# Last products of a three-layer kernel: VectorE's list in another order

## The chip, the cores and the metric

The kernel runs on one core of one Trainium2 chip. The metric is device time in microseconds (us): the time before is the median of three runs. A profile of one further execution shows what each engine of the core did: TensorE (PE, matrix products), VectorE (DVE), ScalarE (ACT), GpSimd (POOL) and SyncE (SP, which issues most DMAs).

## The reference, cut to what matters

```python
q, k, v: (4, 8, 576, 64)      # attention, each row keeps its 32 highest scores
x: (2304, 512)                # its output, then 8 experts of 512 -> 1024 -> 512, the best one per token
def _moe2_ref(x, w_in, w_out, alpha):          # w_in (512, 2048), w_out (2048, 512)
    h = x @ w_in
    g = np.maximum(h, 0.0) + alpha * np.minimum(h, 0.0)
    return (g @ w_out).astype(np.float32)
```

The change touches only this last layer. Its weights arrive in float64 and are turned into float32 on the chip.

## The kernel before

Every float32 operand of a product is held as two tiles, a high part and a low part. ScalarE writes the high part (a copy that rounds), and VectorE or GpSimd subtracts it from the source for the low part. This pair of instructions is called a *split* here. A product is then three matmuls: high by high, high by low, low by high.

The last layer is `last_products`. The 2304 tokens are 9 columns of 256, and the 2048 hidden units are two halves, so there are 18 *groups*, k = 0 to 17: groups 0 to 8 take the first half of the hidden units, groups 9 to 17 the second half. A group has 15 *slots* of 12 matmuls on TensorE:

- eight slots f0 to f7, each of which makes 128 hidden units of the group (`first`): 4 steps d over the 512 inputs, 3 matmuls each. ScalarE (line 1272) and VectorE (line 1273) then apply the slope `alpha`; the pair is called *gg* with its slot's number.
- seven slots for the products of the group before with `w_out`: its 2 by 2 blocks are multiplied with seven products (numbers 1 to 7) and some sums, not with eight. `A[m]` is the split left operand, `B[m]` the split weights of product m. VectorE adds the results (line 1328).

The slots stand in the order `MIXED`: f0, f1, 1, f2, f3, 6, f4, 7, f5, 5, f6, f7, 4, 2, 3. Group 0 has only its eight f slots. Six PSUM banks go round the slots, so a slot needs the bank of six slots earlier to be read out.

Each engine works off its own list in the order of the code; nothing is re-ordered at run time. Around the slots the lists hold:

- the *halves* (lines 1238, 1239): at the end of a group, the split of the next group's input columns, in four pieces; TensorE's next f0 needs the first of them. They stand after gg7, and the last three product slots 4, 2 and 3 run meanwhile.
- the *sums* of a group (lines 1292 to 1295, three instructions on VectorE, after the halves), and s3 (line 1400, at f5); their splits make the `A` tiles (lines 1287 and 1288, the second part on GpSimd).
- `tick`: in groups 1 to 8 it converts 16 pieces of the second half's float64 weights, two pieces a group: four instructions on VectorE (lines 827 to 831), one on GpSimd (line 936). In group 0 it makes the last three splits of `B`.
- `idi`, the token numbers as integers: loaded by a DMA and cast by VectorE in group 0 (line 1385), read by the scatters of the output (line 1315) from group 10 on.
- the *renewal* for the second half: `V`, the split of `w_in`, is written again (`wide_half`, its columns 0 to 511 for slots f0 to f3, 512 to 1023 for f4 to f7), and so are the seven `B` blocks (`new_block`), four of which come from sums of weights (lines 954 to 957, in the order 5, 6, 4, 7).

## Time and profile before

| | before |
|---|---|
| median of 3 runs, us | 1175.03 (1172.89 to 1176.27) |
| the profiled execution: its own time, us | 1173.9 |
| its span, first to last instruction, us | 1172.2 |
| TensorE busy in the span | 1117.1 us, 95% |
| mean granted clock of TensorE (1 is full) | 0.984 |

Times in the rows below are us from the span's start. The profiled execution is 1.1 us below the median of the runs.

### The profile page before, as it was taken

How to read it: one execution, taken by the hardware profiler on the slowest of the kernel's cores; microseconds unless marked ns; L12 is line 12 of the kernel's file. 1: busy time of each engine (PE TensorE's matmuls, PEld its weight loads, DVE VectorE, ACT ScalarE, POOL GpSimd, SP SyncE). 2: the span in 40 equal slices, each digit the busy share in tenths (PEclk: the TensorE clock that was granted, in tenths of full speed). 3: DMA queues.
4: the chain of work that ended last, by engine and by line, in shares of the span. 5: the costliest groups of instructions: out<-in, count | busy, mean ns of one | idle time of the engine just before them, and what ended most of it. 6: DMA issues, size and time to landing. Idle time of an engine off the chain costs nothing.

```text
span 1172.2 us, 28154 instructions
## 1 busy us (share of the span) xinstructions
PE 1117.1 (95%) x9785; PEld 1066.2 (91%) x9785; DVE 872.3 (74%) x3658; ACT 746.0 (64%) x1621; POOL 721.6 (62%) x694
## 2 busy tenths in 40 slices
PE   6999999999999999889999999979999989999996
PEld 4899898899888988889999999979999979999995
DVE  6999989998999899675564666667767797544543
...
GB/s 174 127 131 148 82 78 85 112 79 77 87 85 55 53 26 147 90 189 199 225 191 210 208 247 208 41 101 89 114 92 90 72 46 64 91 73 55 117 30 39
DMA packets 127134, 129.78 MB, mean 111 GB/s; under 512 B 72654, under 2 KB 95182, under 8 KB 126982
## 3 DMA queue, kind: packets, MB, share of 16 engines
...
q0 software_dynamic: 2912, 9.46, 2.2%
q8 instruction: 79, 1.29, 0.5%
q14 instruction: 73, 0.60, 0.2%
...
## 4 chain that ended last, share of the span: by engine, by line
PE 64%; DVE 18%; ACT 9%; issue 4%; DMA 3%; POOL 2%; SPq 0%; POOLq 0%; DVEq 0%; ACTq 0%
PE mm L1327 14%; PE mm L1069 12%; PE mm L1070 11%; PE mm L1068 11%; PE po L345 6%; DVE cand L214 5%; PE s L191 3%; DVE w L236 3%; PE pt L323 2%; ACT sg L285 2%; DVE xT L1239 2%; ACT ss L204 2%; PE pt L324 1%; ACT pT L329 1%; DMA yt<-y 1%
## 5 line engine op out<-in xcount | busy, mean ns | idle before, releaser
L1069 PE MATMUL mm<-xT,wt 128*128 128x256 f32 (+7 forms) x852 | 250.2, 294 | 10.2 <-DVE xT L1239 6.8
L1068 PE MATMUL mm<-xT,wt 128*128 128x256 f32 (+7 forms) x852 | 248.6, 292 | 9.2 <-ACT xT L1238 5.2
L296 POOL TENSOR_TENSOR sg<-ss,sg 128x576 f32<-128x576 f32 x143 | 202.0, 1414 | 84.4 <-ACT sg L285 76.7
L1070 PE MATMUL mm<-xT,wt 128*128 128x256 f32 (+7 forms) x852 | 248.2, 291 | 0.0
L214 DVE MAX8 cand<-ss 128x8 f32<-128x82 f32 (+1 forms) x1008 | 232.3, 234 | 20.0 <-ACT ss L204 19.7
L345 PE MATMUL po<-vt,pT 116*128 116x130 f32 x1440 | 196.2, 282 | 7.4 <-ACT pc L377 6.5
L1327 PE MATMUL mm<-wt,hT 128*128 128x256 f32 x1512 | 193.9, 282 | 0.9 <-POOL hT L1288 0.9
L345 PEld LDWEIGHTS po<-vt,pT 116*128 116x128 f32 x1440 | 172.3, 190 | 22.9 <-ACT pc L377 11.1
L1327 PEld LDWEIGHTS mm<-wt,hT 128*128 128x128 f32 x1512 | 186.2, 191 | 1.1 <-POOL hT L1288 1.1
L1069 PEld LDWEIGHTS mm<-xT,wt 128*128 128x128 f32 x852 | 163.9, 192 | 12.9 <-DVE xT L1239 9.3
L1068 PEld LDWEIGHTS mm<-xT,wt 128*128 128x128 f32 x852 | 163.9, 192 | 9.8 <-ACT xT L1238 5.4
L1070 PEld LDWEIGHTS mm<-xT,wt 128*128 128x128 f32 x852 | 164.0, 192 | 0.0
L323 PE MATMUL pt<-ident,e 128*116 128x128 f32 x720 | 137.5, 275 | 0.7 <-DVE enH L562 0.6
L993 POOL TENSOR_TENSOR wt<-raw,wt 128x1024 fp32r<-128x1024 f32 x29 | 74.7, 2579 | 84.1 <-ACT wt L992 82.3
L285 ACT ACTIVATE sg<-ss,w 128x576 f32<-128x576 f32 x144 | 119.5, 830 | 3.3 <-DVE w L227 2.8
L290 ACT ACTIVATE e<-ss,sm 128x576 f32<-128x576 f32 x144 | 118.7, 824 | 0.1
L191 PE MATMUL s<-kt,qq 64*128 64x144 f32 (+1 forms) x1280 | 113.6, 315 | 5.0 <-ACT ss L204 4.4
L204 ACT ACTIVATE ss<-s 128x576 f32<-128x576 f32 x144 | 102.5, 712 | 14.9 <-PE s L191 9.7
L236 DVE MAX8 w<-sg 128x8 f32<-128x576 f32 x144 | 107.3, 745 | 2.4 <-POOL sg L296 2.1
L1288 POOL TENSOR_TENSOR hT<-wa,hT 128x512 fp32r<-128x512 f32 x36 | 46.5, 1292 | 101.5 <-ACT hT L1287 101.5
L936 POOL TENSOR_TENSOR wf<-wa,raw 128x512 f32<-128x512 f32 x32 | 43.4, 1358 | 99.3 <-DVE raw L831 79.1
L191 PEld LDWEIGHTS s<-kt,qq 64*128 64x128 f32 (+1 forms) x1280 | 80.8, 182 | 24.2 <-ACT ss L204 6.8
...
## 6 DMA issues: line engine op xcount, KB each, us to landing
...
```

What stands on the lines that cost most here:

```text
L191: nc.tensor.matmul(s[to, g, c * n:c * n + n], t["qq"][of, h, q0:q0 + m], t["k"][of, h * HALF + c * n:h * HALF + c * n + n], start=True, st ...
L204: nc.scalar.activation(T.ss.rearrange("p (g s) -> p g s", g=2), T.sv, AF.Copy)
L214: blocks.append(lambda i=i: nc.vector.max(A.cand[:, i], A.ss[:, i * BW:(i + 1) * BW if i + 1 < KB else S]))
L236: fin = [lambda: nc.vector.max(C.w[:, 24:32], C.z), lambda: nc.vector.scalar_tensor_tensor(scr, self.vsel, C.c1, C.w[:, 23:32, None].to_br ...
L285: nc.scalar.activation(T.sg, T.ss, AF.Sign, bias=T.w[:, 23:24], scale=-ABOVE, accum_out=T.c1)
L296: eng.tensor_tensor(T.z, T.ss, T.sg, op=OP.mult)
L323: nc.tensor.matmul(o, T.e[:, c * CK:(c + 1) * CK], self.ident, is_transpose=True, start=True, stop=False)
L345: nc.tensor.matmul(po[:, i:i + 2, :], T.pT[:, c], rhs, start=(c == 0), stop=(c == NCK - 1))
L1068: nc.tensor.matmul(ps, wh, xh, start=first, stop=False)
L1069: nc.tensor.matmul(ps, wh, xl, start=False, stop=False)
L1070: nc.tensor.matmul(ps, wl, xh, start=False, stop=last)
L1327: nc.tensor.matmul(ps, a[:, x, c], b[:, y, c], start=c == r == 0, stop=c == 3 and r == 2)
```

## The change

Four things move; nothing is computed differently, and no instruction of the last layer is added or dropped.

- The cast of the token numbers goes from group 0, f0 to group 1, f0.
- `tick` in group 0 makes its three `B` splits at f2, f4 and f6, not at f2, f5 and f7. In groups 1 to 8 the two weight conversions stand at f1 and f5, not at f3 and f7.
- The renewal of `V` is taken apart: the first columns at f4 and f5 of group 8 (all at f3 before), the second at f0 and f1 of group 9 (all at f7 of group 8, ahead of the sums, before).
- The four sums of weights stand at f0, f2, f4 and f6 of group 9 (all at f0 before), and the splits of the `B` blocks, each right behind the product that last reads the old block before, stand at f3 (B1), f5 (B6) and f6 (B7) of group 9 and at f0 (B5), f2 (B4), f4 (B2) and f6 (B3) of group 10. B1, B6, B7, B2 and B3 are subtracted on GpSimd, B5 and B4 on VectorE (before: B1, B5 and B2 on GpSimd, the other four on VectorE).

```diff
@@ -1273,7 +1273,7 @@
             v.scalar_tensor_tensor(gg, gg, rest[:, 8 * h + f:8 * h + f + 1], ps, op0=OP.mult, op1=OP.add)
             if h == 0:
                 self.n = n1 if g else n0
-                self.tick((g - 1) * 8 + f if g else f, (ng - 1) * 8 if g else 8)
+                self.tick((g - 1) * 8 + (f + 2) % 8 if g else f if f < 7 else -1, (ng - 1) * 8 if g else 7)
             else:
                 self.tick(-1, 1)
 
@@ -1347,21 +1347,29 @@
                 add(at(0, 1), at(0, 1))
                 store(k, 0, 1)
 
-        def wide_half(c):
+        def upper(d, c):
             cs = slice(c * 512, (c + 1) * 512)
-            for d in range(4):
-                t = self.V[d]
-                act.activation(t[:, 0, cs], self.wf[:, d, cs], AF.Copy)
-                (pool if d % 2 else v).tensor_tensor(t[:, 1, cs], self.wf[:, d, cs], t[:, 0, cs].bitcast(F32), op=OP.subtract)
-
-        def new_block(m):
-            if m == 0:
-                for i in (4, 5, 6, 7):
-                    raws[i] = self.wk.tile([P, 4, G2], F32, name="raw", bufs=4)
-                for i, f in self.sums(lambda i: raws[i]):
-                    f()
-                return
-            self.split_block(m, raws[m] if m >= 4 else self.quarter(m), pool if m in (1, 5, 2) else v)
+            t = self.V[d]
+            act.activation(t[:, 0, cs], self.wf[:, d, cs], AF.Copy)
+            (pool if d % 2 else v).tensor_tensor(t[:, 1, cs], self.wf[:, d, cs], t[:, 0, cs].bitcast(F32), op=OP.subtract)
+
+        def new_sum(j):
+            if not raws:
+                raws.update((i, self.wk.tile([P, 4, G2], F32, name="raw", bufs=4)) for i in (5, 6, 4, 7))
+            self.sums(raws.get)[j][1]()
+
+        def new_block(m, eng):
+            self.split_block(m, raws[m] if m >= 4 else self.quarter(m), eng)
+
+        RENEW = {}
+        for d in range(4):
+            RENEW.setdefault((ng - 1, 4 + d // 2), []).append(lambda d=d: upper(d, 0))
+            RENEW.setdefault((ng, d // 2), []).append(lambda d=d: upper(d, 1))
+        for j, f in enumerate((0, 2, 6, 4)):
+            RENEW.setdefault((ng, f), []).append(lambda j=j: new_sum(j))
+        for m, k, f, eng in ((1, 0, 3, pool), (6, 0, 5, pool), (7, 0, 6, pool), (5, 1, 0, v), (4, 1, 2, v), (2, 1, 4, pool),
+                             (3, 1, 6, pool)):
+            RENEW.setdefault((ng + k, f), []).append(lambda m=m, eng=eng: new_block(m, eng))
 
         x = self.load_columns(1)
         for k in range(last + 1):
@@ -1372,8 +1380,6 @@
                 if isinstance(s, int):
                     if k:
                         product(p, s)
-                        if k == ng:
-                            new_block(s)
                     continue
                 f = int(s[1])
                 first(k, t, f)
@@ -1382,9 +1388,8 @@
                         split(5, quarter(p, 1, 0))
                     else:
                         nc.sync.dma_start(ids, self.idc[:NT].rearrange("(t p) -> p t", p=P))
+                    if k == 1:
                         v.tensor_copy(idi, ids)
-                    if k == ng:
-                        new_block(0)
                 if f == 1 and k:
                     split(4, quarter(p, 1, 1))
                 if f == 2 and k:
@@ -1393,8 +1398,6 @@
                     if k:
                         split(3, quarter(p, 0, 0))
                     split(1, quarter(k, 0, 0))
-                    if k == ng - 1:
-                        wide_half(0)
                 if f == 5:
                     s3 = new()
                     v.tensor_tensor(s3, quarter(k, 0, 0), quarter(k, 1, 0), op=OP.subtract)
@@ -1405,9 +1408,9 @@
                     if k < last:
                         t = self.halves(x)
                         x = self.load_columns((k + 2) % ng if k + 2 <= last else ng)
-                    if k == ng - 1:
-                        wide_half(1)
                     sums(k)
+                for renew in RENEW.get((k, f), ()):
+                    renew()
         k = last
         split(5, quarter(k, 1, 0))
         split(4, quarter(k, 1, 1))
```

The first place is VectorE's list in group 0. `xr`, `hT` and `alpha` in the rows of line 1273 are gg; line 967 is the split of a `B` block, line 1239 the halves, line 1400 (1403 in the change) s3. Before:

```order
L1273 SCALAR_TENSOR_TENSOR xr<-xr,alpha,mm 128x256
L1385 CAST idi<-idf 128x18
L1273 SCALAR_TENSOR_TENSOR xr<-xr,alpha,mm 128x256 x2
L967 TENSOR_TENSOR wt<-wf,wt 128x1024
L1273 SCALAR_TENSOR_TENSOR xr<-xr,alpha,mm 128x256
L1273 SCALAR_TENSOR_TENSOR hT<-hT,alpha,mm 128x256 x2
L1400 TENSOR_TENSOR wa<-xr 128x512
L1273 SCALAR_TENSOR_TENSOR hT<-hT,alpha,mm 128x256 x2
L967 TENSOR_TENSOR wt<-wf,wt 128x1024
L1239 TENSOR_TENSOR xT<-xr,xT 128x256 x4
```

and with the change:

```order
L1273 SCALAR_TENSOR_TENSOR xr<-xr,alpha,mm 128x256 x3
L967 TENSOR_TENSOR wt<-wf,wt 128x1024
L1273 SCALAR_TENSOR_TENSOR xr<-xr,alpha,mm 128x256
L1273 SCALAR_TENSOR_TENSOR hT<-hT,alpha,mm 128x256 x2
L1403 TENSOR_TENSOR wa<-xr 128x512
L1273 SCALAR_TENSOR_TENSOR hT<-hT,alpha,mm 128x256
L967 TENSOR_TENSOR wt<-wf,wt 128x1024
L1273 SCALAR_TENSOR_TENSOR hT<-hT,alpha,mm 128x256
L1239 TENSOR_TENSOR xT<-xr,xT 128x256 x4
```

The cast is gone from behind gg0, the first `B` split stays behind gg2, and the last one stands ahead of gg7 instead of behind it.

The second place is VectorE's list at the end of group 1, as in groups 2 to 7: lines 827 to 831 are a weight conversion, `y<-mm` the additions of product results. Before:

```order
L1273 SCALAR_TENSOR_TENSOR wt<-wt,alpha,mm 128x256
L1400 TENSOR_TENSOR wa<-wt 128x512
L1328 TENSOR_TENSOR y<-mm,y 128x256 x2
L1273 SCALAR_TENSOR_TENSOR wt<-wt,alpha,mm 128x256 x2
L827 TENSOR_SCALAR wa<-raw 128x512
L828 SCALAR_TENSOR_TENSOR wa<-raw,wa 128x512
L829 TENSOR_SCALAR raw<-wa 128x512
L831 SCALAR_TENSOR_TENSOR raw<-raw 128x512
L1239 TENSOR_TENSOR xT<-xr,xT 128x256 x4
```

and with the change:

```order
L1273 SCALAR_TENSOR_TENSOR wt<-wt,alpha,mm 128x256
L827 TENSOR_SCALAR wa<-raw 128x512
L828 SCALAR_TENSOR_TENSOR wa<-raw,wa 128x512
L829 TENSOR_SCALAR raw<-wa 128x512
L831 SCALAR_TENSOR_TENSOR raw<-raw 128x512
L1403 TENSOR_TENSOR wa<-wt 128x512
L1328 TENSOR_TENSOR y<-mm,y 128x256 x2
L1273 SCALAR_TENSOR_TENSOR wt<-wt,alpha,mm 128x256 x2
L1239 TENSOR_TENSOR xT<-xr,xT 128x256 x4
```

The conversion stands ahead of s3 and no longer between gg7 and the halves.

The third place is the boundary of groups 8 and 9 on VectorE and on GpSimd. Line 1355 (1354 in the change) is a piece of `V`, lines 954 to 957 are the sums of weights. VectorE before:

```order
L1239 TENSOR_TENSOR xT<-xr,xT 128x256 x4
L1355 TENSOR_TENSOR wt<-wf,wt 128x512 x2
L1292 TENSOR_TENSOR xr<-xr,hT 128x4x128
L1294 TENSOR_TENSOR wa<-xr 128x512
L1295 TENSOR_TENSOR xr<-hT,wa 128x4x128
L1328 TENSOR_TENSOR y<-mm,y 128x256 x3
L1273 SCALAR_TENSOR_TENSOR wt<-wt,alpha,mm 128x256
L954 TENSOR_TENSOR raw<-wf 128x1024
L955 TENSOR_TENSOR raw<-wf,raw 128x1024
L956 TENSOR_TENSOR raw<-wf,raw 128x1024
L957 TENSOR_TENSOR raw<-wf 128x1024
L1273 SCALAR_TENSOR_TENSOR wt<-wt,alpha,mm 128x256 x3
```

and with the change, from the halves on:

```order
L1239 TENSOR_TENSOR xT<-xr,xT 128x256 x4
L1292 TENSOR_TENSOR xr<-xr,hT 128x4x128
L1294 TENSOR_TENSOR wa<-xr 128x512
L1295 TENSOR_TENSOR xr<-hT,wa 128x4x128
L1328 TENSOR_TENSOR y<-mm,y 128x256 x3
L1273 SCALAR_TENSOR_TENSOR wt<-wt,alpha,mm 128x256
L1354 TENSOR_TENSOR wt<-wf,wt 128x512
L954 TENSOR_TENSOR raw<-wf 128x1024
L1273 SCALAR_TENSOR_TENSOR wt<-wt,alpha,mm 128x256
L1354 TENSOR_TENSOR wt<-wf,wt 128x512
L1273 SCALAR_TENSOR_TENSOR wt<-wt,alpha,mm 128x256
L955 TENSOR_TENSOR raw<-wf,raw 128x1024
```

The four sums no longer stand in one piece between gg0 and gg1, and the second columns of `V` come behind gg0 and gg1 of group 9. GpSimd in group 9 before, `hT<-` being the splits of `A` (line 1288) and `wt<-` those of `B` (line 967):

```order
L1288 TENSOR_TENSOR hT<-wa,hT 128x512
L1288 TENSOR_TENSOR hT<-xr,hT 128x512
L1288 TENSOR_TENSOR hT<-hT 128x512
L967 TENSOR_TENSOR wt<-wf,wt 128x1024
L1288 TENSOR_TENSOR hT<-hT 128x512
L1288 TENSOR_TENSOR hT<-xr,hT 128x512
L1288 TENSOR_TENSOR hT<-wt,hT 128x512
L1288 TENSOR_TENSOR hT<-wa,hT 128x512
L967 TENSOR_TENSOR wt<-raw,wt 128x1024
```

and with the change:

```order
L1288 TENSOR_TENSOR hT<-wa,hT 128x512
L1288 TENSOR_TENSOR hT<-xr,hT 128x512
L1354 TENSOR_TENSOR wt<-wf,wt 128x512
L1288 TENSOR_TENSOR hT<-hT 128x512
L1354 TENSOR_TENSOR wt<-wf,wt 128x512
L1288 TENSOR_TENSOR hT<-hT 128x512
L1288 TENSOR_TENSOR hT<-xr,hT 128x512
L1288 TENSOR_TENSOR hT<-wt,hT 128x512
L967 TENSOR_TENSOR wt<-wf,wt 128x1024
L1288 TENSOR_TENSOR hT<-wa,hT 128x512
L967 TENSOR_TENSOR wt<-raw,wt 128x1024 x2
```

Two pieces of `V` and three splits of `B` stand among the splits of `A` there, where two splits of `B` stood before.

## Rows read from the trace of the kernel before

**Rows 1.** the page, part 1: busy us, share of the span, instructions.

```profile
PE 1117.1 (95%) x9785; PEld 1066.2 (91%) x9785; DVE 872.3 (74%) x3658; ACT 746.0 (64%) x1621; POOL 721.6 (62%) x694
```

**Rows 2.** what TensorE waited for, 760 to 1173: us in total, times, longest.

```profile
PE mm L1069 <- DVE xT L1239: 6.8, 12, 1.8
PE mm L1068 <- ACT xT L1238: 5.2, 1, 5.2
PE mm L1068 <- DVE wt L1273: 3.1, 1, 3.1
```

**Rows 3.** the chain that ended last: start, us, engine, tile, line.

```profile
795.69 0.38 PE mm L1069
...
926.84 0.38 PE mm L1069
...
976.20 4.29 PE mm L1327 x36
...
997.50 4.26 PE mm L1327 x36
...
1125.18 4.26 PE mm L1327 x36
```

**Rows 4.** timeline of VectorE, group 0: start, us, instruction, [idle before].

```profile
762.07 0.18 DVE L1385 CAST idi<-idf 128x18 int32<-128x18 f32 x1 [3.64 <-DMA idf<-idc]
...
762.93 1.22 DVE L967 TENSOR_TENSOR wt<-wf,wt 128x1024 fp32r<-128x1024 f32 x1
764.07 0.48 DVE L1273 SCALAR_TENSOR_TENSOR xr<-xr,alpha,mm 128x256 f32<-128x256 f32 x1
...
769.20 2.33 DVE L967 TENSOR_TENSOR wt<-wf,wt 128x1024 fp32r<-128x1024 f32 x1 [0.34 <-ACT wt L966]
771.46 1.42 DVE L1239 TENSOR_TENSOR xT<-xr,xT 128x256 fp32r<-128x256 f32 x4
```

**Rows 5.** timeline of ScalarE and of GpSimd, end of group 0.

```profile
768.11 1.06 ACT L966 ACTIVATE wt<-wf 128x1024 fp32r<-128x1024 f32 x1
...
769.19 1.26 POOL L1288 TENSOR_TENSOR hT<-wa,hT 128x512 fp32r<-128x512 f32 x1
```

**Rows 6.** windows: length, busy of the five engines, granted clock, DMA share, GB/s.

```profile
760.00:776.00 16.00, 8.11 (x49) 7.40 (x49) 11.00 (x19) 6.88 (x15) 5.91 (x4) 0.79 0.47 130
947.75:957.35 9.60, 6.84 (x39) 6.03 (x37) 9.46 (x15) 2.12 (x5) 5.66 (x5) 0.82 0.22 63
967.69:976.20 8.51, 8.51 (x50) 8.51 (x51) 6.04 (x11) 4.73 (x8) 2.83 (x3) 0.66 0.05 17
```

**Rows 7.** timeline of VectorE: end of group 1, end of group 10.

```profile
791.50 0.42 DVE L827 TENSOR_SCALAR wa<-raw 128x512 int32<-128x512 int32 x1
...
793.76 2.55 DVE L1239 TENSOR_TENSOR xT<-xr,xT 128x256 fp32r<-128x256 f32 x4
...
998.36 1.43 DVE L1239 TENSOR_TENSOR xT<-xr,xT 128x256 fp32r<-128x256 f32 x4
```

**Rows 8.** timeline of TensorE and VectorE, groups 8 and 9.

```profile
963.02 1.57 PE L1327 MATMUL mm<-wt,hT 128*128 128x256 f32 x12
...
947.90 4.69 DVE L1239 TENSOR_TENSOR xT<-xr,xT 128x256 fp32r<-128x256 f32 x4
952.51 1.28 DVE L1355 TENSOR_TENSOR wt<-wf,wt 128x512 fp32r<-128x512 f32 x2
...
957.22 2.25 DVE L954 TENSOR_TENSOR raw<-wf 128x1024 f32<-128x1024 f32 x1
```

**Rows 9.** timeline of GpSimd, groups 8 to 10.

```profile
949.44 2.86 POOL L1355 TENSOR_TENSOR wt<-wf,wt 128x512 fp32r<-128x512 f32 x2
...
958.34 2.27 POOL L1288 TENSOR_TENSOR hT<-hT 128x512 fp32r<-128x512 f32 x1
...
976.50 2.41 POOL L967 TENSOR_TENSOR wt<-raw,wt 128x1024 fp32r<-128x1024 f32 x1
...
995.53 1.29 POOL L1288 TENSOR_TENSOR hT<-wa,hT 128x512 fp32r<-128x512 f32 x1 [1.41 <-ACT hT L1287]
```

## The prediction, made before the changed kernel ran

> **What bounds the kernel now.** I read the page first: TensorE is busy 95% of the span [rows 1], so only its idle time, and time at its lower clock, can be won. The waits of TensorE come next: in the last layer it waits for the halves (6.8 and 5.2 us) and for a gg that frees a bank (3.1 us), all written by VectorE or ScalarE; no DMA is among them [rows 2]. Third, the chain that ended last gives the beat. In groups 1 to 7 the chain passes through the second matmul of each f0, held by the halves, six groups in 926.84 - 795.69 = 131.15 us, 21.86 us a group; in groups 10 to 16 the last three products recur in (1125.18 - 997.50) / 6 = 21.28 us [rows 3]. That is the group without waits, and a slot is 21.28 / 15 = 1.42 us. The timelines then show four places where TensorE falls behind this beat:
>
> - The end of group 0: it idles 5.2 and then 1.8 us [rows 2].
> - Seven boundaries, of groups 1 to 8: 0.58 us each, 4.0 us.
> - The boundary of groups 8 and 9: the three slots f0, f1 and product 1 take 9.60 us where 4.26 would do, 5.3 us lost, at a granted clock of 0.82 [rows 6].
> - Inside group 9: from product 7 at 963.02 [rows 8] to product 4 at 976.20 [rows 3] five slots, 7.10 us, take 13.18: 6.1 us lost. 3.1 of them are the bank wait; the rest is time behind it at a mean clock of 0.66 [rows 6].
>
> **The change, place by place.**
>
> *Group 0: gain 3.1.* VectorE waits 3.64 us for the token numbers and casts them in 0.18, ahead of gg1 [rows 4]. All behind it in VectorE's list shifts with it, up to the halves. Without the cast gg3 starts at 764.07 - 3.82 = 760.25. From there on VectorE and ScalarE wait for each other in turn, so the rest of the order counts. At best the last B split also becomes shorter: it took 2.33 us with a GpSimd split beside it and 1.22 with none [rows 4, 5], and the new place has none if GpSimd is done: 3.8 + 1.1 = 4.9 bounds the gain. At worst it stays long, its ScalarE copy (1.06 us [rows 5]) now stands in front of gg7, and s3 doubles (0.7 us more) since GpSimd's other B split lies beside it: 3.8 - 1.06 - 0.7 = 2.0. I laid out the turns: gg3 760.3, ScalarE's copy for the split of product 1, gg4 and a B copy to 762.6, gg5 762.9, s3 to 764.6, its copy, gg6 and a B copy to 766.5, the B subtraction to 767.9, gg7 768.3, first half 768.6. Before, it was ready 771.46 + 1.42 / 4 = 771.8 or so [rows 4]; that is 3.2 to 3.3 us. TensorE still idles over 4 us here, and before it resumed at a lower clock behind such a gap (0.79 on the mean of 760 to 776 [rows 6]); it resumes earlier now, so 0.2 more of that time falls on matmuls. I take 3.1, range 2.0 to 4.9. The cast costs 0.18 us in group 1, under TensorE's work; its reader is nine groups off.
>
> *Seven boundaries: gain 4.0.* The conversion before the halves runs from 791.50 to 793.76, 2.26 us, and the halves behind it take 2.55 us since GpSimd's part of the conversion lies beside them; where nothing does, they take 1.43 [rows 7]. With the change nothing stands between gg7 and the halves. What is late next? At f5 the conversion delays s3, s3 holds ScalarE's queue (its split's copy), and behind that stand gg6, gg7 and the halves. f5 ends 12.8 us into the group and gg5 1.0 later; conversion 2.3 and s3 0.7 to 1.3 bring 17.3, the copy and two gg 19.1, the first half 19.5. TensorE wants it at 21.3: 1.9 us in hand. At f1 the conversion delays gg2 and the two additions behind it, under six banks (8.5 us). So all of 7 x 0.58 = 4.0 comes back; lower bound 3.0. SP's list moves as well: two weight loads of a group are now issued ahead of the store of product 5 and of the next columns' load. Each waits for a buffer that the conversion four pieces before has freed, so nothing queues behind them, and the columns' load comes earlier because the halves do; I cost this at nothing. If a load were late, the halves would be, and the 1.9 us is the cover.
>
> *Boundary of groups 8 and 9: gain 5.1.* Before, the halves ran 4.69 us beside GpSimd's 2.86 us of V [rows 8, 9]. Now the V pieces stand two and two behind f4 and f5. By the sum above, with ScalarE's two V copies and one V subtraction of 0.64 to 1.2 us more (1.28 for two alone [rows 8]), the halves start 21.2 us into the group and the first is ready at 21.5, 0.2 late; then they come as fast as TensorE takes them. 5.3 - 0.2 = 5.1; with GpSimd beside the halves, as before the change at other boundaries, 1.3 less.
>
> *Group 9: gain 1.6.* The sums no longer stand in one block (from 957.22 on [rows 8]) but in four places, so gg1 no longer frees its bank late. But f4 to f7 need V's second columns, written in group 9 now. GpSimd cannot start before the sums of group 8 are there: the halves end 1.3 us into group 9, two of the sums and ScalarE's copy follow, so 3.2 us in (an estimate). Then it has three splits of A and two pieces of V, 3 x 1.29 + 2.86 = 6.7 us [rows 9]: 9.9, where f4 wants the last piece at 6 x 1.42 + 1.06 = 9.6. That is 0.3 late with GpSimd undisturbed. In the same stretch VectorE has two V pieces and one weight sum, 2 x 0.64 + 1.2 = 2.5 us alone, and these two kinds slow each other: the first sum took 2.25 us [rows 8], against 1.22 for another 128 x 1024 subtraction with GpSimd idle [rows 4], and GpSimd's split beside the sums took 2.27 against 1.29 [rows 9]. If they only take turns, the last piece comes 2.8 late. Nearest to these rows is nearly taking turns: 2.5 us. Behind the 3.1 us wait the lower clock cost another 3.0; behind 2.5 I take 2.0 (between none and 3.0). So 4.5 of the 6.1 stay. Bounds: 0.3 stays (gain 5.8), or a loss of 10.5 (gain -4.4, second rival).
>
> The Trainium skill has a rule on this that speaks against the change: "SBUF — State Buffer", section "Who interferes with whom", says that a VectorE instruction with two SBUF inputs and a GpSimd instruction that reads SBUF exclude each other for their whole length. By the strict rule the wait at f4 would be 2.8, by GpSimd undisturbed 0.3. The rows of the sums agree with it almost fully; the split of 1.26 us that ran beside the 2.33 us B subtraction [rows 4, 5] shows one side alone paying.
>
> *Group 10: -0.3.* B3 is subtracted by GpSimd (2.41 us [rows 9]) behind f6; product 3 follows four slots behind f6's end, at 19.9. f6 ends at 15.8, ScalarE's gg and copy bring 17.2, GpSimd 19.7, and the halves lie beside it: 0 to 0.8 late, I take 0.3.
>
> **Sum.** 3.1 + 4.0 + 5.1 + 1.6 - 0.3 = 13.5. The profiled execution took 1173.9 us in all, span 1172.2; 1173.9 - 13.5 = 1160.4. The median is 1.1 higher, which gives 1161.5; I predict 1161.
>
> **The rivals.**
>
> *Group 9 is clear (1155.5).* If GpSimd is undisturbed, 0.3 stays and no clock drop follows: gain 5.8 instead of 1.6, and 1175.0 - 17.7 = 1157.3; with the best case of group 0 as well, 1155.5. For it: the halves beside GpSimd's work slowed VectorE alone. Against: the sums, where both paid.
>
> *GpSimd and VectorE take turns through all of group 9 (1167.5).* GpSimd's list for the group is 7 x 1.29 + 2.86 + 3 x 2.41 = 19.1 us [rows 9]; VectorE's two-input instructions are four sums, two V pieces, s3, halves and the group's sums, 4.9 + 1.3 + 0.7 + 1.4 + 2.1 = 10.4. That is 29.5 in a group of 21.3: 8.2 over. Before it was 25.4, 4.1 over, and 6.1 was lost. Were all 8.2 due within the group, with 2.3 us of lower clock, 10.5 would be lost, 4.4 more than before: 1175.0 - 7.5 = 1167.5. Against: B6, B7 and two splits of A, 7.4 us, are due only in group 10. This is what the skill's page named above would give if the deadlines did not help.
>
> *Group 0 does not get shorter (1164.6).* The change would not do there what moving a 3.64 us wait suggests, if the turns of VectorE and ScalarE end on something else, such as the columns' load. Against: what releases TensorE there is ScalarE and VectorE, no DMA [rows 2].
>
> *The conversions stall every group (1179, slower).* At f5 the conversion stands ahead of s3, and ScalarE's queue behind s3. If conversion and s3 take over 1.9 us longer than above, each first-half boundary stalls. At twice their time (3.6 us more, as with the halves beside GpSimd) each is 1.7 us late; with 0.8 of lower clock behind it (a quarter of group 9's 3.0) seven boundaries lose 17.5 where they lost 4.0, the other places gain 9.5, and 1175.0 + 13.5 - 9.5 = 1179.0. It decides from (9.5 + 4.0) / 7 = 1.9 us lost a boundary on. Against it: GpSimd waits for the conversion, so it is idle beside it.
>
> **How the numbers follow.** Forecast 0.60 (its own range 1157 to 1165), group 9 clear 0.12, taking turns 0.16, group 0 unchanged 0.05, conversions stall 0.04; 0.03 for a gain that is met by a loss I don't see, within the noise. The range 1155 to 1168 holds all but the last 0.07 and some of the edges. A change under 0.3% (3.5 us) can't be told from none here. Faster 0.93, same 0.03, slower 0.04.
>
> **What would show it.** Right: no wait for the token numbers in group 0, and the first half ready near 768.6; groups 1 to 7 at 21.28 us; the wait of TensorE at f0 of group 9 under 0.5 us; a wait of about 2.5 us for V at f4 of group 9, with a lower clock behind it. Wrong: a wait for the halves in groups 1 to 8, f4 of group 9 without a wait or over 4 us late, a bank wait in group 9, or product 3 of group 10 waiting for B3.

## The result, and the profile of the changed kernel

The changed kernel takes 1164.31 us (median of 4 runs, 1162.65 to 1166.24), the kernel before 1174.38 us beside it (4 runs, 1172.89 to 1176.27): a ratio of 0.9914, with a 95% interval of 0.9891 to 0.9937, or 10.1 us less. 1161.0 was predicted, with a range of 1155 to 1168. The profiled execution took 1165.06 us with a span of 1163.4, 8.8 us less than the 1172.2 of before.

The page, part 1, of the changed kernel (columns as in [rows 1]): TensorE has the same 9785 instructions and is busy for 3.9 us less.

```profile
PE 1113.2 (96%) x9785; PEld 1064.3 (91%) x9785; DVE 864.7 (74%) x3656; ACT 747.1 (64%) x1621; POOL 729.6 (63%) x696
```

What TensorE waits for in the last layer of the changed kernel, the view of [rows 2]:

```profile
PE mm L1069 <- DVE xT L1239: 5.3, 3, 4.2
PE mm L1068 <- ACT xT L1238: 5.1, 2, 4.9
PE mm L1327 <- POOL hT L1288: 0.9, 1, 0.9
PE mm L1070 <- POOL wt L1354: 0.5, 1, 0.5
PE mm L1070 <- DVE wt L1354: 0.5, 1, 0.5
```

The twelve waits for VectorE's halves have become three, but their sum has only gone from 6.8 to 5.3 us, since one of them is 4.2 us long; the bank wait of 3.1 us is gone. The timeline of TensorE (start, us, instruction, [idle before <- releaser]) says where they stand:

```profile
767.79 0.58 PE L1068 MATMUL mm<-xT,wt 128*128 128x256 f32 x1 [4.89 <-ACT xT L1238]
769.20 0.58 PE L1069 MATMUL mm<-xT,wt 128*128 128x256 f32 x1 [0.83 <-DVE xT L1239]
...
941.62 0.38 PE L1069 MATMUL mm<-xT,wt 128*128 128x256 f32 x1 [0.29 <-DVE xT L1239]
...
951.73 0.38 PE L1070 MATMUL mm<-xT,wt 128*128 128x256 f32 x1 [0.47 <-DVE wt L1354]
...
952.87 0.39 PE L1070 MATMUL mm<-xT,wt 128*128 128x256 f32 x1 [0.52 <-POOL wt L1354]
...
964.82 0.38 PE L1068 MATMUL mm<-xT,wt 128*128 128x256 f32 x1 [0.22 <-ACT xT L1238]
...
969.36 0.58 PE L1069 MATMUL mm<-xT,wt 128*128 128x256 f32 x1 [4.16 <-DVE xT L1239]
```

The first two are f0 of group 1, as before. Between 769 and 941, over seven boundaries, there is no wait. At the end of group 1, for one, the halves now start behind gg7, in VectorE's timeline:

```profile
789.29 1.97 DVE L1239 TENSOR_TENSOR xT<-xr,xT 128x256 fp32r<-128x256 f32 x4
```

They are done at 791.3, and f0 of group 2 begins, behind the last three products, at 792.1. 941.62 is f0 of group 9, late by 0.29. At f4 of group 9 TensorE waits for the pieces of V, 0.47 and 0.52 us. The last row is new: a wait of 4.16 us for the halves at f0 of group 10.

The chain that ended last, the view of [rows 3], gives the beat and the cost of groups 8 and 9:

```profile
787.99 4.26 PE mm L1327 x36
...
915.67 4.26 PE mm L1327 x36
...
922.77 1.43 PE mm L1327 x12
...
974.51 1.43 PE mm L1327 x12
...
995.79 1.43 PE mm L1327 x12
```

The last three products of groups 1 to 7 now recur in (915.67 - 787.99) / 6 = 21.28 us, the group without waits, where it was 21.86 before. 922.77, 974.51 and 995.79 are product 1 in groups 8, 10 and 11: from group 8 to group 10 it takes 51.74 us, 9.2 more than two groups of 21.28; from 10 to 11 exactly one.

**A table for all kernels below.** The start of product 1 is taken from the timeline of TensorE in each group. The second column is that start in group 1, counted from VectorE's slope instruction (line 1251), with which the last layer begins; the others are what was lost against 21.28 us a group. The boundary of groups 8 and 9 is from product 1 of group 8 to that of group 9, and so on.

| kernel | product 1 of group 1 | seven boundaries | boundary 8 and 9 | group 9 | group 10 | last three together |
|---|---|---|---|---|---|---|
| before | 18.64 | 4.05 | 5.00 | 6.29 | 0.00 | 11.3 |
| changed | 16.29 | 0.01 | 0.58 | 8.60 | 0.00 | 9.2 |
| e1, cast alone | 15.26 | 4.01 | 4.56 | 5.61 | 0.85 | 11.0 |
| e2, conversions back | 16.28 | 3.93 | 2.09 | 8.79 | 0.47 | 11.4 |
| e12, conversions alone | 18.42 | 0.00 | 0.00 | 9.20 | 0.04 | 9.2 |
| e10, old group 9 | 16.56 | 0.00 | 0.00 | 9.24 | 0.00 | 9.2 |
| e11, old group 9, exact | 16.93 | 0.46 | 0.00 | 8.35 | 0.88 | 9.2 |
| e5, old splits of group 0 | 15.55 | 0.39 | 0.54 | 8.71 | 0.49 | 9.7 |
| e7, later splits of group 0 | 11.94 | 0.43 | 0.55 | 8.71 | 0.40 | 9.7 |
| e3, fourth sum later | 16.24 | 0.00 | 0.57 | 7.25 | 0.52 | 8.3 |
| e4, B6 and B7 later | 16.29 | 0.00 | 0.58 | 2.35 | 4.73 | 7.7 |
| e6, group 9 relieved | 15.93 | 0.00 | 0.54 | 1.49 | 4.44 | 6.5 |
| e8, e6 and e7 | 12.26 | 0.12 | 0.55 | 1.53 | 4.47 | 6.6 |
| e9, e8 with B4 ahead of s3 | 12.20 | 0.19 | 0.55 | 1.54 | 3.70 | 5.8 |

Of before and the changed kernel it says: 2.35 us come from group 0, 4.04 from the seven boundaries, 4.42 from the boundary of groups 8 and 9, and 2.31 are lost in group 9. That is 8.5; with 0.3 us by which the slope instruction came earlier (757.35 after, 757.66 before), it is the 8.8 of the spans.

Each row is one profile. In the changed kernel, e5 and e7 the lists of groups 8 to 10 are the same, and the three places lose 9.2, 9.7 and 9.7 us, so a difference of 0.5 there can't be told from none. The slope instruction begins between 755.03 (e12) and 759.45 (e5), though no edit moves anything ahead of it; the times of the runs contain that scatter, the table does not.

### The profile page after: what moved, and what is told of

Same layout as the page of the kernel before. It is cut to its first block, busy times and chain, and to the rows that moved or that the text cites. A ratio compares the mean times of both kernels' runs of the same rounds, so it can differ in the third digit from the quotient of the medians.

```text
span 1163.4 us, 28142 instructions
## 1 busy us (share of the span) xinstructions
PE 1113.2 (96%) x9785; PEld 1064.3 (91%) x9785; DVE 864.7 (74%) x3656; ACT 747.1 (64%) x1621; POOL 729.6 (63%) x696
## 3 DMA queue, kind: packets, MB, share of 16 engines
q8 instruction: 79, 1.29, 0.5%
## 4 chain that ended last, share of the span: by engine, by line
PE 66%; DVE 14%; ACT 11%; issue 4%; DMA 3%; POOL 2%; POOLq 0%; SPq 0%; DVEq 0%; ACTq 0%
PE mm L1327 14%; PE mm L1069 12%; PE mm L1070 12%; PE mm L1068 12%; PE po L345 6%; DVE cand L214 3%; PE s L191 3%; ACT sg L285 3%; PE pt L323 2%; DVE w L236 2%; ACT ss L204 2%; ACT pT L329 2%; PE pt L324 1%; POOL sg L296 1%; ACT e L290 1%
## 5 line engine op out<-in xcount | busy, mean ns | idle before, releaser
L214 DVE MAX8 cand<-ss 128x8 f32<-128x82 f32 (+1 forms) x1008 | 229.6, 231 | 20.6 <-ACT ss L204 20.2
L345 PEld LDWEIGHTS po<-vt,pT 116*128 116x128 f32 x1440 | 172.2, 190 | 23.1 <-ACT pc L377 11.3
```

Source lines behind the costliest of these rows:

```text
L214: blocks.append(lambda i=i: nc.vector.max(A.cand[:, i], A.ss[:, i * BW:(i + 1) * BW if i + 1 < KB else S]))
L345: nc.tensor.matmul(po[:, i:i + 2, :], T.pT[:, c], rhs, start=(c == 0), stop=(c == NCK - 1))
```

## What held group 9, and group 0

The lists of the changed kernel around the new wait. VectorE, timeline (start, us, instruction, [idle before]):

```profile
941.15 1.42 DVE L1239 TENSOR_TENSOR xT<-xr,xT 128x256 fp32r<-128x256 f32 x4
...
947.64 2.32 DVE L954 TENSOR_TENSOR raw<-wf 128x1024 f32<-128x1024 f32 x1
...
959.19 2.16 DVE L1403 TENSOR_TENSOR wa<-wt 128x512 f32<-128x512 f32 x1
...
963.67 3.16 DVE L956 TENSOR_TENSOR raw<-wf,raw 128x1024 f32<-128x1024 f32 x1
...
967.14 3.17 DVE L1239 TENSOR_TENSOR xT<-xr,xT 128x256 fp32r<-128x256 f32 x4
```

GpSimd and ScalarE beside it:

```profile
957.42 3.38 POOL L967 TENSOR_TENSOR wt<-wf,wt 128x1024 fp32r<-128x1024 f32 x1
...
963.35 5.67 POOL L967 TENSOR_TENSOR wt<-raw,wt 128x1024 fp32r<-128x1024 f32 x2
```

```profile
961.39 0.64 ACT L1287 ACTIVATE hT<-wa 128x512 fp32r<-128x512 f32 x1 [4.88 <-DVE wa L1403]
```

At the boundary of groups 8 and 9 the halves take 1.42 us (941.15), since GpSimd does nothing there. At the end of group 9 they take 3.17. GpSimd subtracts B6 and B7 from 963.35 to 969.02, and VectorE's fourth sum (963.67) and the first piece of the halves, 0.36 us by itself (1.42 / 4), both stand beside these two: TensorE gets its piece at 969.3, when B7 is done. Earlier in the group B1's subtraction (957.42, 3.38 us) lies beside s3 (2.16 us), for which ScalarE waits 4.88 us, with the copies of B6 and B7 and its own halves behind that.

The Trainium skill, "SBUF — State Buffer", section "Who interferes with whom", says that a VectorE instruction with two SBUF inputs and a GpSimd instruction that reads SBUF lock each other out, and that the loser blocks until the other instruction is done. By that rule the halves cannot pass B7's subtraction, and the trace agrees: 969.02 against 969.36 for TensorE's matmul.

The granted clock behind the wait, by the view of windows (columns as in [rows 6]):

```profile
969.40:976.00 6.60, 6.60 (x37) 6.60 (x38) 6.14 (x12) 3.30 (x7) 2.95 (x3) 0.63 0.55 154
```

TensorE is busy through all of this stretch, at 0.63 on the mean, which lies between its two levels (1.2 and 2.4 GHz, 0.5 and 1), so that 6.60 x 0.37 = 2.4 us of its work fell away. The waits of group 9 (0.47 + 0.52 + 0.22 + 4.16 = 5.4) and this make 7.8 of the 8.6 us.

Group 0 of the changed kernel, VectorE's timeline and GpSimd's:

```profile
757.35 0.16 DVE L1251 TENSOR_SCALAR alpha<-alpha 128x16 f32<-128x16 f32 x1
...
763.01 2.27 DVE L1403 TENSOR_TENSOR wa<-xr 128x512 f32<-128x512 f32 x1
...
767.19 1.22 DVE L967 TENSOR_TENSOR wt<-wf,wt 128x1024 fp32r<-128x1024 f32 x1 [0.46 <-ACT wt L966]
768.33 0.47 DVE L1273 SCALAR_TENSOR_TENSOR hT<-hT,alpha,mm 128x256 f32<-128x256 f32 x1
768.72 1.42 DVE L1239 TENSOR_TENSOR xT<-xr,xT 128x256 fp32r<-128x256 f32 x4
...
772.84 0.70 DVE L1392 CAST idi<-idf 128x18 int32<-128x18 f32 x1
```

```profile
762.38 2.35 POOL L967 TENSOR_TENSOR wt<-wf,wt 128x1024 fp32r<-128x1024 f32 x1
```

The wait for the token numbers of [rows 4] is gone, the last B split is short (1.22 us, 2.33 before), and the halves start at 768.72 instead of 771.46. But s3 takes 2.27 us beside GpSimd's B split.

## The experiments

Every time stands beside runs of the kernel before on the same chip, in brackets; the change itself had 0.9914.

**e1: the cast alone.** The kernel before, with one edit:

```diff
                         nc.sync.dma_start(ids, self.idc[:NT].rearrange("(t p) -> p t", p=P))
+                    if k == 1:
                         v.tensor_copy(idi, ids)
```

> The kernel before with one edit: the cast of the token numbers in group 1, f0. Theory (the DMA wait of 3.64 us shifts everything behind it in VectorE's list): all of group 0's chain up to the first half comes 3.8 us earlier, the first half is ready near 768 us, TensorE's two waits there (5.2 and 1.8) fall together by 3.5 to 3.8, nothing else moves, time about 1171. Rival (the turns of VectorE and ScalarE, the B splits among them, set the end of group 0): the waits fall by under 2 us.

1170.24 us [1173.57], ratio 0.9975 (0.9962 to 0.9988). The two waits at f0 of group 1, in the timeline of TensorE:

```profile
764.18 0.58 PE L1068 MATMUL mm<-xT,wt 128*128 128x256 f32 x1 [2.52 <-ACT xT L1238]
...
766.58 0.58 PE L1069 MATMUL mm<-xT,wt 128*128 128x256 f32 x1 [1.81 <-DVE xT L1239]
```

The halves start 10.0 us behind the slope instruction, 13.8 before: all of the 3.8 us of the stall and the cast is passed on. The two waits fall from 6.97 to 4.33 us, by 2.64: more than the rival's 2 us, which falls, but less than the 3.5 to 3.8 expected. The rest of it is a third wait, inside group 0, for a bank that the delayed gg1 had to read out. It is gone in e1 and in the changed kernel; TensorE's timeline of the kernel before has it:

```profile
762.68 0.38 PE L1068 MATMUL mm<-xT,wt 128*128 128x256 f32 x1 [0.91 <-DVE xr L1273]
```

Product 1 of group 1 comes 3.4 us earlier (15.26 against 18.64), more than in the changed kernel (16.29). So the new places of the splits of group 0 cost 1.0 us there; e5 tests that.

**e5: the old places of group 0's splits.** The changed kernel with

```diff
-                self.tick((g - 1) * 8 + (f + 2) % 8 if g else f if f < 7 else -1, (ng - 1) * 8 if g else 7)
+                self.tick((g - 1) * 8 + (f + 2) % 8 if g else f, (ng - 1) * 8 if g else 8)
```

> The changed kernel with the three B splits of group 0 back at f2, f5 and f7. Theory (what the change gained in group 0 is the cast's 3.8 us; the splits' new places gave back about 1.4, since s3 then runs beside GpSimd's B2 and the last split's ScalarE copy stands ahead of gg7): the first half begins 10.0 us after VectorE's slope instruction, as with the cast alone, and not 11.4; time 1 to 1.5 us under the changed kernel. Rival (the new places did no harm, the difference is chance): 11.4 again and the same time.

1164.23 us [1172.58], 0.9926 (0.991 to 0.9943): no gain in time. The halves do start 10.0 us behind the slope instruction, as in e1, and product 1 of group 1 comes 0.74 us earlier (15.55 against 16.29), but of that only 0.36 is left by the next product (20.20 against 20.56). The table has 0.39 us for it under the seven boundaries. What became of the rest shows in the windows from the first matmul of f0 of group 1 to product 6, in the changed kernel and in e5 (columns as in [rows 6]):

```profile
767.79:777.91 10.12, 9.29 (x60) 9.00 (x61) 8.55 (x17) 4.48 (x11) 3.28 (x3) 0.75 0.33 105
767.52:779.65 12.13, 10.11 (x60) 9.91 (x61) 9.53 (x16) 4.47 (x11) 4.53 (x4) 0.72 0.28 95
```

TensorE starts f0 2.4 us earlier in e5 (8.07 against 10.44 from the slope instruction) and then takes 2.0 us longer over the same five slots: 1.2 in the second wait (2.02 against 0.83), and 0.8 in which it is busy longer (10.11 against 9.29 us), at a lower mean clock. So 1.4 us on VectorE (11.4 from the slope instruction to the halves in the changed kernel) became 0.4 on TensorE and nothing in the time; the gain that was expected did not come.

**e7: two splits of group 0 moved out of it.** The changed kernel, B1's split kept at f2 and B2's and B3's made behind f0 of group 1:

```diff
-                self.tick((g - 1) * 8 + (f + 2) % 8 if g else f if f < 7 else -1, (ng - 1) * 8 if g else 7)
+                self.tick((g - 1) * 8 + (f + 2) % 8 if g else -1 if f != 2 else 0, (ng - 1) * 8 if g else n0)
...
+        def rest_of_blocks():
+            self.n = n0
+            for at in range(1, n0):
+                self.step -= 1
+                self.tick(at, n0)
+
+        RENEW[1, 0] = [rest_of_blocks]
```

> The changed kernel with the splits of B2 and B3 out of group 0, at f0 of group 1. Theory (the turns of VectorE and ScalarE set the end of group 0; two ScalarE copies of 1.06 us and one VectorE split stand in them): the first half begins about 7.6 us after VectorE's slope instruction instead of 11.4, TensorE's waits at f0 of group 1 fall from 5.7 to about 2 us, time 3 to 5 us under the changed kernel. Rival (something else, such as the columns' load, is then late): the wait stays over 4 us.

1160.1 us [1172.58], 0.9892 (0.9875 to 0.9908). In its timeline of TensorE, f0 of group 1:

```profile
764.03 0.38 PE L1068 MATMUL mm<-xT,wt 128*128 128x256 f32 x1 [1.57 <-ACT xT L1238]
...
764.81 0.39 PE L1069 MATMUL mm<-xT,wt 128*128 128x256 f32 x1 [0.40 <-DVE xT L1239]
```

The halves start 7.3 us behind the slope instruction, and product 1 of group 1 4.35 us earlier than in the changed kernel. The matmuls behind these shorter waits take 0.38 and 0.39 us each; behind the 4.89 us wait of the changed kernel, and the 2.52 of e1, the row shows 0.58. The length of the wait alone does not decide that: e5's matmul behind 2.52 us takes 0.38, and e9's behind 0.39 us takes 0.58. From f0 to product 6 the granted clock is 0.82 on the mean:

```profile
764.03:773.42 9.39, 8.99 (x61) 8.79 (x61) 7.76 (x11) 6.15 (x13) 5.24 (x4) 0.82 0.62 225
```

The time is 4.2 us below the changed kernel's by the medians and 2.6 by the ratios, against 3 to 5 expected. So what held group 0 was VectorE's and ScalarE's work in front of the halves, the B splits among it.

**e2: the conversions back at f3 and f7.** The changed kernel with

```diff
-                self.tick((g - 1) * 8 + (f + 2) % 8 if g else f if f < 7 else -1, (ng - 1) * 8 if g else 7)
+                self.tick((g - 1) * 8 + f if g else f if f < 7 else -1, (ng - 1) * 8 if g else 7)
```

> The changed kernel with the weight conversions back at f3 and f7 of groups 1 to 8. Theory (a conversion between gg7 and the halves delays the halves past the cover of three product slots): groups 1 to 7 take 21.86 us again, 4.0 us in all, and the boundary of groups 8 and 9 waits 1 us or more, so time about 1169 to 1170. Rival (with the rest of the list changed the halves have room enough): 21.28 us a group, time as the changed kernel.

1171.23 us [1173.57], 0.9978 (0.9968 to 0.9988). Its waits for the halves on VectorE, against three in the changed kernel:

```profile
PE mm L1069 <- DVE xT L1239: 8.8, 11, 4.2
```

The seven boundaries lose 3.9 us again, 0.56 each, as the theory says; the boundary of groups 8 and 9 loses 2.1 instead of 0.6. All the rest of the change, without the conversions, is worth 2.3 us.

**e12: the conversions alone.** The kernel before with

```diff
-                self.tick((g - 1) * 8 + f if g else f, (ng - 1) * 8 if g else 8)
+                self.tick((g - 1) * 8 + (f + 2) % 8 if g else f, (ng - 1) * 8 if g else 8)
```

> The kernel before with one edit: the weight conversions of groups 1 to 17 stand behind f1 and f5 instead of f3 and f7; the cast, the splits of group 0, the V pieces, sums and B splits stay as before. Theory (the conversions, with the cast, are all of the gain): 4.0 us at the seven boundaries and 4.5 at that of groups 8 and 9, of which 2.9 are given back in group 9, as in e10_old_group9; 5.6 us, 0.9952 of before, near 1167.5 us. Rival (the parts need each other: without the spread V pieces and sums the boundary of groups 8 and 9 stays late): only the 4.0 us of the seven boundaries or less, over 3 us lost at that boundary, 0.9966 or more of before.

1165.63 us [1172.38], 0.9943 (0.993 to 0.9957): 6.75 us. (The conversions stand only in groups 1 to 8, so the edit reaches no later group.) The theory had 5.6; the rival falls. The seven boundaries lose nothing, and neither does the boundary of groups 8 and 9, though the pieces of V and the sums stand where they stood. But group 9 loses 9.2 us, 2.9 more than before. Its timeline of VectorE shows the halves at that boundary, with no conversion in front of them and none of GpSimd's V pieces beside their beginning (4.69 us before [rows 8]):

```profile
939.77 1.97 DVE L1239 TENSOR_TENSOR xT<-xr,xT 128x256 fp32r<-128x256 f32 x4
```

and its timeline of TensorE the waits of group 9:

```profile
947.65 0.39 PE L1068 MATMUL mm<-xT,wt 128*128 128x256 f32 x1 [2.38 <-DVE y L1328]
...
959.01 0.58 PE L1068 MATMUL mm<-xT,wt 128*128 128x256 f32 x1 [3.98 <-DVE wt L1273]
```

Both are waits for a PSUM bank that VectorE reads late: an addition that stands behind the V pieces, and a gg behind the block of sums. What the boundary gained has in part gone into the group: 5.0 us less there, 2.9 more here.

**e10: the old group 9 in the changed kernel.** The V pieces as two blocks of four, the sums as one, the B splits behind their products:

```diff
-        for d in range(4):
-            RENEW.setdefault((ng - 1, 4 + d // 2), []).append(lambda d=d: upper(d, 0))
-            RENEW.setdefault((ng, d // 2), []).append(lambda d=d: upper(d, 1))
-        for j, f in enumerate((0, 2, 6, 4)):
-            RENEW.setdefault((ng, f), []).append(lambda j=j: new_sum(j))
+        for c in (0, 1):
+            RENEW[ng - 1, (4, 7)[c]] = [lambda c=c: [upper(d, c) for d in range(4)]]
+        RENEW[ng, 0] = [lambda: [new_sum(j) for j in range(4)]]
...
                         product(p, s)
+                        if k == ng:
+                            new_block(s, pool if s in (1, 5, 2) else v)
```

> The changed kernel with the V pieces, sums of weights and B splits of groups 8 to 10 put back where they stood before the change (all four V pieces of a half behind f4 and f7, the four sums as one block behind f0 of group 9, each B split behind the product that used the block last); the cast, the conversions and the splits of group 0 stay as changed. Theory (spreading them won 4.4 us at the boundary of groups 8 and 9 and lost 2.3 us inside group 9): 2.1 us slower than the changed kernel, 1166.4 us, 0.9935 of before; the bank wait of 3.1 us at product 4 of group 9 is back, and no wait for the halves at f0 of group 10 over 0.3 us. Rival (the old boundary was late because of the conversion in front of the halves as well, which is gone now): the boundary loses 3 us instead of 5, and the time is within 0.5 us of the changed kernel's 1164.3 us.

1163.42 us [1172.84], 0.9929 (0.9915 to 0.9942). The theory, that the spreading had won 4.4 us at the boundary and lost 2.3 in group 9, falls: the boundary loses nothing without it, group 9 loses 9.2 with the old lists, and the three places together 9.2, as in the changed kernel. The time does not tell the two apart: by the medians it is 0.9 us below the 1164.3 of the rival, but the ratio of 0.9929 lies between the theory's 0.9935 and the 0.9914 of the change. The rival's 3 us at the boundary don't come either. The two waits in its timeline of TensorE are those of e12:

```profile
946.12 0.38 PE L1068 MATMUL mm<-xT,wt 128*128 128x256 f32 x1 [2.54 <-DVE y L1328]
...
957.32 0.58 PE L1068 MATMUL mm<-xT,wt 128*128 128x256 f32 x1 [3.83 <-DVE wt L1273]
```

**e11: the same, with V ahead of the sums.** In e10 the second block of V pieces stood behind the sums of group 8's products; here it stands ahead of them, where it stood before:

```diff
-            RENEW[ng - 1, (4, 7)[c]] = [lambda c=c: [upper(d, c) for d in range(4)]]
+            RENEW[ng - 1, (4, 70)[c]] = [lambda c=c: [upper(d, c) for d in range(4)]]
...
+                    for renew in RENEW.get((k, 70), ()):
+                        renew()
                     sums(k)
```

> The run with the old group 9 (e10_old_group9) with the second four V pieces of group 8 ahead of the sums of its products, where they stood before the change, instead of behind them. It tells what cleared the boundary of groups 8 and 9 there. Theory (the conversion in front of the halves was the cause, since it put the halves beside GpSimd's V pieces): the halves still start without a conversion, the first half is on time, under 0.8 us are lost at the boundary, and the time is within 1.5 us of 1163.4 us. Rival (V pieces ahead of the sums delay the halves by themselves): 3 us or more are lost at the boundary, a wait for the halves of over 1.5 us at f0 of group 9, and 1166 us or more.

1164.04 us [1172.38], 0.9923 (0.991 to 0.9937). No loss at the boundary, 9.2 us in the three places together: it is the conversion that the halves had to wait for, and the rival, by which V ahead of the sums delays them, falls.

**e3: the fourth sum later.** The changed kernel with the sum of line 956 at f1 of group 10:

```diff
-        for j, f in enumerate((0, 2, 6, 4)):
-            RENEW.setdefault((ng, f), []).append(lambda j=j: new_sum(j))
+        for j, (e, f) in enumerate(((0, 0), (0, 2), (1, 1), (0, 4))):
+            RENEW.setdefault((ng + e, f), []).append(lambda j=j: new_sum(j))
```

> The changed kernel with the fourth sum of weights at f1 of group 10, so that no sum stands between gg6 and gg7 of group 9. It tells apart what made TensorE wait 4.2 us for the first half at f0 of group 10. List theory (the sum of 3.16 us stands ahead of gg7 and the halves in VectorE's list): the wait falls to under 1 us. Lock theory (the first half could not run beside GpSimd's splits of B6 and B7, which end at 969.0 whatever stands ahead on VectorE): they end under 1 us earlier, the wait stays at 3 us or more.

1163.52 us [1173.57], 0.9916 (0.9898 to 0.9933). The waits at f0 of group 10 sum to 2.97 us instead of 4.38, at the edge of the lock theory (3 us or more) and far from the list theory's 1 us: taking the sum away brings the halves forward (963.25, its timeline of VectorE), but not past GpSimd's B6 and B7 (961.72, its timeline of GpSimd).

```profile
963.25 4.29 DVE L1239 TENSOR_TENSOR xT<-xr,xT 128x256 fp32r<-128x256 f32 x4
```

```profile
961.72 4.88 POOL L967 TENSOR_TENSOR wt<-raw,wt 128x1024 fp32r<-128x1024 f32 x2
```

**e4: B6 and B7 later.** The changed kernel with these two splits, still on GpSimd, at f0 and f1 of group 10:

```diff
-        for m, k, f, eng in ((1, 0, 3, pool), (6, 0, 5, pool), (7, 0, 6, pool), (5, 1, 0, v), (4, 1, 2, v), (2, 1, 4, pool),
+        for m, k, f, eng in ((1, 0, 3, pool), (6, 1, 0, pool), (7, 1, 1, pool), (5, 1, 0, v), (4, 1, 2, v), (2, 1, 4, pool),
```

> The changed kernel with the splits of B6 and B7 at f0 and f1 of group 10 instead of f5 and f6 of group 9; both are due behind f3 and f4 of group 10. Lock theory: with GpSimd idle the fourth sum takes 1.2 us and the halves 1.4, the wait at f0 of group 10 falls under 0.5 us, 4 to 6 us are won with the lower clock behind it, time about 1159. List theory: the sum still stands ahead of the halves, but shorter; a wait of 1 to 2 us is left. A loss at products 6 and 7 of group 10 would show GpSimd late there.

1163.84 us [1173.57], 0.9917 (0.9899 to 0.9936). The halves at the end of group 9, in its timeline of VectorE:

```profile
964.86 1.42 DVE L1239 TENSOR_TENSOR xT<-xr,xT 128x256 fp32r<-128x256 f32 x4
```

With GpSimd idle beside them they take 1.42 us and TensorE waits 0.60 for them: it was B6 and B7. But the 1159 us expected did not come: product 6, product 7 and one of the last three of group 10 now wait for their splits, in its timeline of TensorE:

```profile
973.40 1.56 PE L1327 MATMUL mm<-wt,hT 128*128 128x256 f32 x11 [0.70 <-POOL wt L967]
...
978.95 1.56 PE L1327 MATMUL mm<-wt,hT 128*128 128x256 f32 x11 [2.46 <-POOL wt L967]
...
989.90 0.39 PE L1327 MATMUL mm<-wt,hT 128*128 128x256 f32 x1 [0.78 <-POOL wt L967]
```

**e6: group 9 relieved.** The changed kernel with B6 and B7 subtracted by VectorE, all splits but B1's spread over group 10, and two of the sums at other slots:

```diff
-        for j, f in enumerate((0, 2, 6, 4)):
-            RENEW.setdefault((ng, f), []).append(lambda j=j: new_sum(j))
-        for m, k, f, eng in ((1, 0, 3, pool), (6, 0, 5, pool), (7, 0, 6, pool), (5, 1, 0, v), (4, 1, 2, v), (2, 1, 4, pool),
-                             (3, 1, 6, pool)):
+        for j, (e, f) in enumerate(((0, 1), (0, 2), (1, 3), (0, 4))):
+            RENEW.setdefault((ng + e, f), []).append(lambda j=j: new_sum(j))
+        for m, k, f, eng in ((1, 0, 3, pool), (6, 1, 0, v), (7, 1, 1, v), (5, 1, 2, v), (4, 1, 5, v), (2, 1, 3, pool),
+                             (3, 1, 4, pool)):
```

> The changed kernel with less for GpSimd and VectorE together in group 9: B6 and B7 on VectorE at f0 and f1 of group 10, the fourth sum at f3 of group 10, B5 at f2, B4 at f5, B2 and B3 on GpSimd at f3 and f4 of group 10, the first sum behind V's pieces at f1 of group 9. Lock theory (the two engines' work adds up, and a 128 x 1024 subtraction holds them 2.4 us on GpSimd but 1.2 on VectorE): no wait over 0.6 us at f0 or at a product of group 10, the wait for V at f4 of group 9 under 0.7, time about 6 us under the changed kernel, 1158. Rival (the work is only shifted, as with B6 and B7 on GpSimd in group 10): waits of 3 us or more at the products or the halves of group 10, under 2 us won.

1162.85 us [1172.58], 0.9918 (0.9902 to 0.9935). The wait for the halves is gone and group 9 loses 1.5 us instead of 8.6, but group 10, which had lost nothing, loses 4.4. The profile of this run shows 3 us less in the last layer than the changed kernel, and the runs' ratio no difference from it; the 6 us expected did not come, and the rival is nearer. The wait for V at f4 of group 9 is 1.25 us, where under 0.7 was expected. The new place is B4, behind an s3 that takes 2.23 us (0.68 alone) beside two of GpSimd's splits, and product 4 waits 1.27 + 1.31 us for it; timelines of VectorE and of GpSimd:

```profile
978.32 2.23 DVE L1403 TENSOR_TENSOR wa<-xr 128x512 f32<-128x512 f32 x1
```

```profile
977.59 5.18 POOL L967 TENSOR_TENSOR wt<-wf,wt 128x1024 fp32r<-128x1024 f32 x2
```

**e8: e6 and e7 together.** The edits of both.

> The edits of the two kernels e6 and e7 together. Theory: their gains add, since they lie nine groups apart: about 1154. If one of the two does nothing, 1158 to 1160.

1157.82 us [1172.58], 0.9879 (0.9863 to 0.9896), faster than both kernels. It is not the 1154 expected, and lies at the edge of "one of the two does nothing" (1158 to 1160). In the table, though, the parts add: from the slope instruction to group 11 e7 is 3.45 us shorter than the changed kernel, e6 3.08 and e8 6.55. The 1154 would have needed the 6 us expected of e6.

**e9: B4 ahead of s3.** e8 with

```diff
-        for j, (e, f) in enumerate(((0, 1), (0, 2), (1, 3), (0, 4))):
+        for j, (e, f) in enumerate(((0, 2), (0, 3), (1, 3), (0, 4))):
             RENEW.setdefault((ng + e, f), []).append(lambda j=j: new_sum(j))
-        for m, k, f, eng in ((1, 0, 3, pool), (6, 1, 0, v), (7, 1, 1, v), (5, 1, 2, v), (4, 1, 5, v), (2, 1, 3, pool),
-                             (3, 1, 4, pool)):
+        for m, k, f, eng in ((1, 0, 3, pool), (6, 1, 0, v), (7, 1, 1, v), (5, 1, 2, v), (4, 1, 4, v), (2, 1, 3, pool),
+                             (3, 1, 5, pool)):
```

> The run with both later splits (e8_both) with three further moves: the B4 split at f4 of group 10 (ahead of s3, which stands at f5), B3's split on GpSimd at f5 instead of f4, and the first two sums of weights one tile later (f2 and f3 of group 9), behind the upper V pieces. Theory (what was lost at product 4 of group 10, 1.18 + 1.31 us, came from B4 standing behind an s3 of 2.2 us beside GpSimd, and the V wait of 1.25 us from a sum of weights beside GpSimd's V piece): no wait over 0.3 us at product 4, the wait for V at f4 of group 9 under 0.7 us, and 1154.5 us, 3.3 less than e8_both. Rival (the two engines' total work in groups 9 and 10 has no room left, so a loss only moves): a new wait of 1.5 us or more in group 10 or at f0 of group 11, and 1157 to 1159 us.

1155.86 us [1172.84], 0.9854 (0.9839 to 0.9869), the fastest of all: 17.0 us below before. It lies between the two theories. The wait for B4 is gone, but its timeline of TensorE has a new one, for B3, which GpSimd now subtracts behind the split of s3 (until 981.27), and the wait for V at f4 of group 9 is still 1.25 us; the three places lose 5.8 us, 0.8 less than in e8.

```profile
981.32 1.88 PE L1327 MATMUL mm<-wt,hT 128*128 128x256 f32 x11 [1.94 <-POOL wt L967]
```

## Why the prediction was right, and where it was wrong

The time lies in the range and 3.3 us above the value. Step by step:

- *Group 0: 3.1 predicted, 2.35 measured.* The mechanism holds (e1: the whole 3.8 us stall is passed on to the halves). The turns were laid out nearly as they ran: gg7 ended at 768.33 + 0.47 = 768.8 for 768.3, the first half was ready at 768.72 + 1.42 / 4 = 769.1 for 768.6. The size is off by these 0.5 us, since s3 took 2.27 us beside GpSimd's split (0.71 before), a slowdown that stood only in the lower bound and at 0.7 us there, and by 0.3 because the slope instruction came that much earlier.
- *Seven boundaries: 4.0 predicted, 4.04 measured.* Right, and shown twice, by taking the conversions' move away (e2, 3.9 us lost again) and by making it alone (e12, none lost).
- *Boundary of groups 8 and 9: 5.1 predicted, 4.42 measured.* The size is nearly right, its cause is not, so that the size came out is luck. The step named the V pieces, put two and two behind f4 and f5. With V, sums and splits where they stood before, the boundary loses nothing (e10 to e12). What mattered was the conversion in front of the halves: with it the halves began late enough for GpSimd's V pieces to lie beside them. The spread pieces help only where the conversion stays (2.1 us lost in e2, 4.6 in e1), and there group 9 takes it back (8.8 against 5.6). With the conversion gone the boundary of the changed kernel still loses 0.6 and that of e10 to e12 nothing; that the pieces' copies and subtractions ahead of the halves make the difference is not tested by itself.
- *Group 9: a gain of 1.6 predicted, a loss of 2.3 measured.* This is the term that failed. The wait at f4 was 0.99 us instead of 2.5; 4.5 of the 6.1 us were to stay, and 8.6 were lost. The step took the deadline of V at f4 for the group's only tight place. The second rival was argued away with "B6, B7 and two splits of A, 7.4 us, are due only in group 10". They are, but GpSimd starts them as soon as their sources are there, and that is beside VectorE's fourth sum and the halves, which are due. e4 shows it: with B6 and B7 elsewhere the halves take 1.42 us and the wait falls from 4.38 to 0.60.
- *Group 10: -0.3 predicted, 0.00 measured.* B3 is in time.

The three errors of size go one way, and in the profiles 8.8 us were gained where 13.5 were predicted. The medians show 10.1, since the profiled execution of before lay 0.5 us below its median and that of the changed kernel 0.75 above; that brought the time nearer to the value. None of the signs of being wrong that the prediction lists came either: the place that failed, the halves at f0 of group 10, was not among them.

So the rival of two engines that take turns had the right mechanism in group 9; its 10.5 us lost were 8.6. "Group 9 is clear" falls with the 4.16 us wait, "group 0 does not get shorter" with e1, and "the conversions stall every group" with seven boundaries that lose 0.01 us.

**Where the gain comes from.** The cast alone is worth 3.3 us by the medians (e1), the conversions alone 6.75 (e12): 10.1 together, what the changed kernel gains. By the table the two are 3.7 and 6.3, 10.0 together, and the change 8.5. No run has just these two; e10 and e11, which have them and the new splits of group 0, are at 0.9929 and 0.9923, inside the interval of the change. Spreading the V pieces, the sums and the splits brings nothing that these runs can tell from zero: with the old conversions the three places lose 11.3 and 11.0 us without the spreading and 11.4 with it (before, e1, e2), with the new ones 9.2 without it (e10, e11, e12) and 9.2 to 9.7 with it (the change, e5, e7).

That these sums are equal does not make the order there indifferent. e6 has as many B splits on each engine as the old lists, three on GpSimd and four on VectorE, and all its pieces inside the same three places, but loses 6.5 us where e10, e11 and e12 lose 9.2. e4 keeps the engines of the changed kernel and only puts two splits a few slots later, and loses 7.7 for 9.2 to 9.7. So order alone was worth 1.5 to 2.7 us. No run hands a split to the other engine and leaves its place, so what that is worth is not shown by itself.

The total of both lists may still set a floor. An estimate from the prediction's prices, over groups 9 and 10 of the changed kernel: GpSimd 14 x 1.29 + 2.86 + 5 x 2.41 = 33.0 us, VectorE's instructions of two inputs 4.9 + 1.3 + 2 x 1.22 + 2 x (0.7 + 1.4 + 2.1) = 17.0, together 7.4 us more than the 42.6 of two groups; with three B splits on GpSimd and four on VectorE it is 5.1 more. The least that was lost in these two groups is 7.1 with the first division (e4) and 5.2 with the second (e9). That fits, but it is an inference; no run took a part of this work away altogether.
